# Issuing the loads of a cached attention kernel from GpSimd's DMA queue instead of SyncE's

## The chip, the core and the metric

The kernel runs on one core of one Trainium2 chip. The metric is the device time of one execution in microseconds, the median of several runs. A profile of one further execution says what each engine and each DMA queue did, and when. The engines are TensorE (PE; its weight loads are PEld), VectorE (DVE), ScalarE (ACT), GpSimd (POOL) and SyncE (SP), which here only issues DMAs.

## What is computed

One token attends over a cache of 65,536 keys and values for each of 8 key-value heads, with 2 query heads to each, and the result is mixed with a small MLP by a gate.

```python
q = (x @ wq).reshape(B, Sq, 16, 256)          # x is 1 x 448
scores = einsum(q, k_cache) * (256 ** -0.5)   # k_cache: 8 heads x 65536 x 256, bf16
a = (softmax(scores) @ v_cache).reshape(B, Sq, 4096) @ wo
h = layernorm(x)
b = gelu(h * w1 + b1) @ w2 + b2               # per channel, F = 1792
g = sigmoid((x * gate_w).sum(-1))
return g * a + (1 - g) * b
```

The two caches are 268 MB each and are read once; everything else is small.

## The kernel before

The 65,536 positions of each head are cut into 4 passes, so there are 32 passes (`NP`), four to a head (`PPH`). A pass takes 16,384 keys and the same number of values: 8 MB each, with 128 partitions and 64 KB of contiguous memory for each partition. A pass of keys is worked on in 8 steps (`BODY`) of 2,048 keys; the first four steps (`DC`) use the upper half of the keys' tile (`HV` to `NV`), the last four the lower half.

**The passes on TensorE.** In each step of `keys`, TensorE transposes 16 tiles of keys (line 359, `kst<-ident,kring`, as 32-bit pairs), VectorE (line 675) and ScalarE (line 820) copy them to `ktT`, and TensorE multiplies them with the query (line 380, `sps<-qcur,ktT`). The transposes count up `sem_tr`; `sem_tr[NB - 1]` is what the loads of keys wait for. After a pass's scores come the maximum (`maxima`, lines 397 and 399 on TensorE), the exponentials on ScalarE, and then `values` (line 411, `acc<-vbuf,pT`), 128 matmuls of weights with values, the last of which counts up `sem_pv`. In passes 0 and 1 the values of a pass are used right behind its keys; from pass 2 (`LEAD`) on, keys run one pass ahead of values. After four passes a head is finished: its output is multiplied with its part of wo (line 472, `project`, counting up `s_proj`).

**Buffers.** `kring` holds one pass of keys and a half, `vbuf` holds one pass of values. Before the first values arrive, `vbuf` holds wq and other early data, so that the first value load waits until the query is made (`s_q`, `s_hb`). Each later value load waits for the value matmuls before it (`sem_pv`), each key load for the transposes of the buffer half that it overwrites.

**Queues.** SyncE issues, in an order written out by hand in `block.sync`: the first wo, two pieces of wq, and both 4 MB halves of the first keys (`sem_k` for the upper half, `sem_kb` for the lower); then a loop over the passes with one load of keys and one of values in turn, a wo load after each finished head (`load_wo`, line 261), and at the end the last values in five pieces, the last wo in two and the store of the output. All cache loads go through one helper, `load`, whose DMA is line 269. Around `LEAD` the keys are loaded in halves and quarters, some with semaphores of their own (`sem_kc`, `sem_kq`). ScalarE issues six small loads at the start (lines 780 to 785). GpSimd makes the identity and the ones, then waits for the two quarter loads (`sem_kq`) and adds 16 to `sem_k` on their behalf.

**Waits on TensorE.** At the first step of a pass (`transposes`, `k == 0`, line 346) it waits for `sem_k` at 16 times the number of the pass; at the fifth step for `sem_kb` and, in three passes, for one of `sem_kc`. Before a projection it waits for `sem_wo`.

Of the kernel before, what the change touches and what calls it, by code (L numbers as in the profile page):

```python
# [7 lines left out]
AF = mybir.ActivationFunctionType  # L8
ALU = mybir.AluOpType
AX = mybir.AxisListType  # L10


def bass_gated_mix__gqa_block_cached__mixer_token_mlp__decode_kernel(
# [17 lines left out]
    H = A_k_cache.shape[1]  # L31
    T = A_k_cache.shape[2]
    DH = A_k_cache.shape[3]
    DM = A_x.shape[-1]
    HQ = A_wq.shape[1] // DH
    REP = HQ // H
# [9 lines left out]
    DC = 4  # L46
    NB = NT // 4
    NCPH = T // CH
    NC = H * NCPH
    BODY = 2 * DC  # L50
    NV = BODY * NT
    NP = NC // BODY
    PPH = NCPH // BODY
# [10 lines left out]
    LEAD = 2  # L64
    assert LEAD % 2 == 0 and 1 < LEAD < PPH
    NLATE = 112
    NRING = 72
    pieces = [(0, NRING), (NRING, 96), (96, NLATE), (NLATE, 124), (124, NV)]
# [16 lines left out]
    HV = NV // 2  # L85
# [11 lines left out]
    with ctx:  # L97
# [6 lines left out]
        def new_sem(name):  # L104
            return ctx.enter_context(nc.semaphore(name))

        kring = sb([P, NV + HV, DH], bf16, "kring")
        kring_f = kring.bitcast(f32)
        vbuf = sb([P, NV, DH], bf16, "vbuf")
# [10 lines left out]
        wo_sb = sb([P, REP, 2 * DM], bf16, "wo_sb")  # L120


        wo_rows = wo_sb[:, :, :].rearrange("p h n -> p (h n)")
# [73 lines left out]

        sem_k = new_sem("sem_k")
        sem_kb = new_sem("sem_kb")
        sem_kc = [new_sem("sem_kc%d" % i) for i in range(3)]  # L200
        sem_kq = [new_sem("sem_kq%d" % i) for i in range(2)]
        sem_v = new_sem("sem_v")
        sem_vp = [new_sem("semvp%d" % i) for i in range(len(pieces))]
# [3 lines left out]
        sem_wo = new_sem("sem_wo")  # L207
# [6 lines left out]
        sem_pv = new_sem("sem_pv")  # L214
# [37 lines left out]
        def src(cache, j, n0=0, n1=NV):  # L252
            g, m = divmod(j, PPH)
            s = cache[0, g, m * BODY * CH:(m + 1) * BODY * CH, :].rearrange("(p n) d -> p n d", p=P)
            return s[:, n0:n1, :].rearrange("p n d -> p (n d)")

        @block.sync
        def _(eng):
            def load_wo(g):
                w = A_wo[g * REP * DH:(g + 1) * REP * DH, :]  # L260
                eng.dma_start(wo_rows, w.rearrange("(p i) n -> p (i n)", i=2 * REP)).then_inc(sem_wo, 16)

            load_wo(0)
            eng.dma_start(wq_a.rearrange("p j n -> p (j n)"),
                          A_wq[0:WF * P, :].rearrange("(p j) n -> p (j n)", p=P)).then_inc(sem_wq, 16)
            eng.dma_start(wq_b, A_wq[WF * P:DM, :].rearrange("r (a n) -> (r a) n", a=2)
                          ).then_inc(sem_wq, 16)
            def load(dst, cache, j, n0, n1, at, sem):
                eng.dma_start(dst[:, at + n0:at + n1, :].rearrange("p n d -> p (n d)"), src(cache, j, n0, n1)
                              ).then_inc(sem, 16)  # L270

            load(kring, A_k_cache, 0, HV, NV, 0, sem_k)
            load(kring, A_k_cache, 0, 0, HV, 0, sem_kb)

            def load_v(j):
                if j == 0:
                    eng.wait_ge(s_q, 1)
                    eng.wait_ge(s_hb, 1)
                else:
                    eng.wait_ge(sem_pv, j)  # L280
                load(vbuf, A_v_cache, j, 0, NV, 0, sem_v)
                g, m = divmod(j, PPH)
                if m == 0 and 1 <= g < H - 1:
                    eng.wait_ge(s_proj, g)
                    load_wo(g)

            for j in range(NP):
                if j == LEAD + 1:
                    eng.wait_ge(sem_tr[NB - 1], BODY * LEAD)
                    load(kring, A_k_cache, j, HV, NV, HV, sem_kc[1])  # L290
                    eng.wait_ge(sem_tr[NB - 1], BODY * LEAD + DC // 2)
                    load(kring, A_k_cache, j, 0, HV // 2, HV, sem_kq[0])
                if j >= 1:
                    eng.wait_ge(sem_tr[NB - 1], BODY * (j - 1) + DC)
                if j == LEAD:
                    load(kring, A_k_cache, j, HV, NV, 0, sem_k)
                    load(kring, A_k_cache, j, 0, HV, 0, sem_kc[0])
                elif j == LEAD + 1:
                    load(kring, A_k_cache, j, HV // 2, HV, HV, sem_kq[1])
                elif j == NP - 1:  # L300
                    load(kring, A_k_cache, j, 0, HV, HV, sem_k)
                    load(kring, A_k_cache, j, HV, NV, HV, sem_kc[2])
                elif j >= 1:
                    load(kring, A_k_cache, j, 0, NV, HV * (j % 2), sem_k)
                if j < LEAD:
                    load_v(j)
                elif j > LEAD:
                    load_v(j - 1)


            for (n0, n1), sem in zip(pieces, sem_vp):
                if n0 == 0:
                    eng.wait_ge(sem_tr[NB - 1], BODY * (NP - 1) + DC)
                elif n0 == NRING:
                    eng.wait_ge(sem_pv, NP - 1)
                load(kring if n1 <= NRING else vbuf, A_v_cache, NP - 1, n0, n1, 0, sem)
            eng.wait_ge(s_proj, H - 1)
            for h in range(REP):
                w = A_wo[(HQ - REP + h) * DH:(HQ - REP + h + 1) * DH, :]
                eng.dma_start(wo_sb[:, h, :], w.rearrange("(p j) n -> p (j n)", j=2)).then_inc(sem_wl[h], 16)  # L320
            eng.wait_ge(s_fin, NCG)
            eng.dma_start(out_ap, out_row[:, :]).then_inc(sem_out, 16)
            eng.wait_ge(sem_out, 16)

        @block.gpsimd
        def _(eng):
            eng.memset(ident[:, :], 0.0)
            eng.drain()
            eng.affine_select(
                out=ident[:, :], in_=ident[:, :], compare_op=ALU.not_equal, fill=1.0,  # L330
                base=0, pattern=[[-1, P]], channel_multiplier=1,
            )
            eng.drain()
            eng.memset(ones_sq[:, :], 1.0).then_inc(sem_ident, 1)
            for sem in sem_kq:
                eng.wait_ge(sem, 16)
            eng.sem_inc(sem_k, 16)

        @block.tensor
        def _(pe):  # L340
# [2 lines left out]

            def transposes(k, c, j, u16, x2):
                if k == 0:
                    pe.wait_ge(sem_k, u16)
                if k == DC:
                    pe.wait_ge(sem_kb, 16)
                    for p, sem in zip((LEAD, LEAD + 1, NP - 1), sem_kc):
                        with pe.If(j == p):  # L350
                            pe.wait_ge(sem, 16)

                done = pe.snap(c + 1, min_val=1, max_val=NC)

                def tiles(at):
                    for b in range(NB):
                        pe.wait_ge(sem_ev[b], done)
                        for i in range(4):
                            ins = pe.transpose(kst[:, b, i * P:(i + 1) * P],  # L359
                                               kring_f[:, at + NT * (k % DC) + 4 * b + i, :], ident[:, :])  # L360
                        ins.then_inc(sem_tr[b], 1)

                if k < DC:
                    tiles(HV)
                else:
                    with pe.If(x2 == 0):
                        tiles(0)
                    with pe.Else():
                        tiles(NV)
# [165 lines left out]
            pe.reg_mov(m_reg, 0)  # L535
            g_reg = pe.alloc_register("g_reg")
            pe.reg_mov(g_reg, 1)
            with nc.Fori(0, NP + 1, 1, engines=on, head_slot={pe.engine: 0}) as jj:
                j = pe.snap(jj, min_val=0, max_val=NP)
                m = pe.snap(m_reg, min_val=0, max_val=PPH)  # L540
# [4 lines left out]
                    maxima(pe.snap(j, min_val=1, max_val=NP))  # L545
                with pe.If(j < NP):
                    c0 = pe.snap(j * BODY, min_val=0, max_val=NC)
                    u16 = pe.snap(j * 16 + 16, min_val=16, max_val=16 * NP)
                    keys(c0, j, u16, pe.snap(x2_reg, min_val=0, max_val=NV))
                with pe.Else():  # L550
                    pe.wait_ge(s_mix, 1)
# [16 lines left out]
                with pe.If(m >= PPH):  # L568
                    with pe.If(j < NP):
                        g1 = pe.snap(g - 1, min_val=1, max_val=H)  # L570
                        pe.wait_ge(s_cp, g1)
                        clear(acc[:, 0:NACC])
                        by_row(acc[:, SELC:NACC]).then_inc(s_sel, 1)
                        pe.wait_ge(sem_wo, pe.snap(g * 16 - 16, min_val=16, max_val=16 * H))
                        pe.wait_ge(s_oTn, g1)
                        project(range(2 * REP)).then_inc(s_proj, 1)
                        pe.reg_mov(m_reg, 0)
# [281 lines left out]
```

## Time and profile before

| | |
|---|---|
| runs | 1263.95, 1264.36, 1264.56 us; median 1264.36 us |
| span of the profiled execution (first to last instruction) | 1262.8 us |
| time of the profiled execution beside its span | not given on the page; its span stands 1.6 us below the median of the runs |
| mean granted TensorE clock | 0.842 |
| HBM read | 544.22 MB |
| DMA packets | 12,197, of which 1,433 are under 512 B |

The span is the profile's; the runs are timed as a whole. Rows of groups give the line, the engine, the operation, output and inputs, how often, the busy time with the mean duration, and the idle time before it with what ended it. Rows of waits give the total, the number and the longest. Rows of DMA issues give the transfer, the issuing queue, how often, the size where the page has it, and the median time from issue to landing. "x1" and the like is a count.

### The profile page before, as it was taken

To read this page: it belongs to the slowest core of one execution; us is meant where nothing else is said; L and a number is where in the kernel's file an instruction comes from. 1 tells how busy PE (TensorE), PEld (TensorE's weight loads), DVE (VectorE), ACT (ScalarE), POOL (GpSimd) and SP (SyncE) were. 2 spreads that over 40 slices of the span, in tenths; PEclk is the share of its full clock that TensorE was granted. 3 is DMA by queue.
4 is the path that set the end of the run, shared out by engine and by line. 5 is a ranking of instruction groups with operands and counts; after the bars stand their busy time and mean duration, and the time that the engine had idled before them with its cause. 6 is when DMAs were issued, how large, how long until landed. Compare 5 with 4: busy or idle time off the path is not lost.

```text
span 1262.8 us, 39606 instructions
## 1 busy us (share of the span) xinstructions
PE 974.4 (77%) x17019; PEld 891.1 (71%) x17019; DVE 498.3 (39%) x1126; ACT 545.7 (43%) x692; POOL 0.9 (0%) x7
## 2 busy tenths in 40 slices
PE   4768887678777797776977678886778866798787
PEld 3667876678667687666877667876668766687685
DVE  3234434344444435444354433342333432334342
ACT  2344643345433455343454334443344433445352
POOL 0000000000000000000000000000000000000000
PEclk8878888898877888788888889887798877888787
DMA  9999999999999999999999999999999999999998
GB/s 415 433 421 426 439 436 436 432 432 432 432 434 440 436 432 432 432 430 438 434 434 429 437 434 432 432 432 436 436 436 432 432 432 432 432 434 438 428 438 370
DMA packets 12197, 544.35 MB, mean 431 GB/s; under 512 B 1433, under 2 KB 1692, under 8 KB 2972
## 3 DMA queue, kind: packets, MB, share of 16 engines
q1 hardware_dynamic: 12098, 544.22, 99.8%
q8 instruction: 6, 0.10, 0.0%
q10 hardware_dynamic: 90, 0.01, 0.0%
q14 instruction: 3, 0.02, 0.0%
HBM read 544.22 MB, written 0.00 MB: 431 GB/s over the span
## 4 chain that ended last, share of the span: by engine, by line
DMA 58%; PE 37%; DVE 2%; issue 2%; DVEq 0%; SPq 0%; ACT 0%
DMA kring<-in_A_k_cache_dram 55%; PE kst L359 26%; PE sps L380 6%; PE acc L411 3%; DMA vbuf<-in_A_v_cache_dram 2%; DMA wo_sb<-in_A_wo_dram 1%; PE acc L461 0%; PE sps L399 0%; PE prj L472 0%; DVE ktT L675 0%; ACT z_b L825 0%; PE acc L404 0%; DVE accs L709 0%; PE sps L397 0%; DVE mrow L686 0%
## 5 line engine op out<-in xcount | busy, mean ns | idle before, releaser
L359 PE MATMUL kst<-ident,kring 128*128 128x128 f32 x4096 | 565.0, 299 | 181.4 <-DMA kring<-in_A_k_cache_dram 158.2
L359 PEld LDWEIGHTS kst<-ident,kring 128*128 128x128 f32 x4096 | 513.1, 156 | 190.7 <-issue 184.6
L820 ACT ACTIVATE ktT<-kst 128x1024 bf16<-128x1024 bf16 x512 | 499.9, 1021 | 337.2 <-PE kst L359 336.8
L675 DVE COPY ktT<-kst 128x1024 bf16<-128x1024 bf16 x512 | 353.9, 692 | 435.5 <-PE kst L359 409.4
L380 PEld LDWEIGHTS sps<-qcur,ktT 128*128 128x128 bf16 x8192 | 238.0, 97 | 2.6
L380 PE MATMUL sps<-qcur,ktT 128*128 128x2 bf16 x8192 | 236.6, 163 | 0.0
L411 PE MATMUL acc<-vbuf,pT 128*2 128x256 bf16 x4008 | 164.1, 341 | 4.6 <-issue 3.3
L411 PEld LDWEIGHTS acc<-vbuf,pT 128*2 128x2 bf16 x4008 | 113.5, 103 | 47.0 <-issue 4.5
L803 ACT ACTIVATE fade<-mdif 128x2 f32<-128x2 f32 x32 | 6.5, 203 | 305.1 <-DVE mdif L692 305.1
L686 DVE TENSOR_REDUCE mrow<-sps 2x1 f32<-2x128 f32 x32 | 8.9, 279 | 162.6 <-PE sps L397 162.6
L399 PEld LDWEIGHTS sps<-mdiag,mones 2*128 2x128 f32 x64 | 11.1, 216 | 27.9 <-DVE mdiag L688 27.9
L397 PE MATMUL sps<-ident,mcol 128*2 128x128 f32 x32 | 8.9, 279 | 27.9 <-issue 26.4
L399 PE MATMUL sps<-mdiag,mones 2*128 2x2 f32 x64 | 13.9, 284 | 21.3 <-DVE mdiag L688 21.3
L807 ACT ACTIVATE pT<-sps,mneg 128x64 f32 x128 | 30.3, 334 | 0.0
L825 ACT ACTIVATE z_b<-z_b 128x448 bf16<-128x448 bf16 x14 | 8.1, 576 | 48.2 <-DVE z_b L662 48.2
L404 PE MATMUL acc<-pT,ones_sq 128*128 128x32 bf16 x256 | 12.0, 182 | 21.9 <-issue 18.4
L397 PEld LDWEIGHTS sps<-ident,mcol 128*2 128x2 f32 x32 | 2.6, 80 | 36.6 <-issue 28.3
L709 DVE COPY accs<-acc 128x288 f32<-128x288 f32 x8 | 3.7, 458 | 61.7 <-PE acc L411 61.7
L681 DVE TENSOR_REDUCE mcol<-sps 128x2 f32<-128x256 f32 x32 | 13.5, 423 | 34.6 <-PE sps L380 34.6
L404 PEld LDWEIGHTS acc<-pT,ones_sq 128*128 128x128 bf16 x256 | 8.8, 99 | 26.0 <-issue 22.4
L704 DVE TENSOR_SCALAR acc<-acc,fader 128x256 f32<-128x256 f32 x32 | 15.8, 493 | 2.5
L691 DVE TENSOR_SCALAR mneg<-sps 128x2 f32<-128x2 f32 x32 | 5.1, 160 | 16.8 <-PE sps L399 16.8
(113 smaller groups left out, 168.8 us busy)
## 6 DMA issues: line engine op xcount, KB each, us to landing
kring<-in_A_k_cache_dram SPq DMA_DIRECT2D x7, 4096.0 KB, 25.2
kring<-in_A_v_cache_dram SPq DMA_DIRECT2D x1, 4608.0 KB, 25.4
kring<-in_A_k_cache_dram SPq DMA_DIRECT2D x2, 2048.0 KB, 13.1
wo_sb<-in_A_wo_dram SPq DMA_DIRECT2D x7, 448.0 KB, 25.3
vbuf<-in_A_wq_dram SPq DMA_DIRECT2D x1, 3072.0 KB, 10.8
vbuf<-in_A_v_cache_dram SPq DMA_DIRECT2D x1, 1536.0 KB, 8.1
vbuf<-in_A_v_cache_dram SPq DMA_DIRECT2D x1, 1024.0 KB, 10.2
vbuf<-in_A_v_cache_dram SPq DMA_DIRECT2D x1, 768.0 KB, 11.6
```

The source lines that it names most:

```text
L359: ins = pe.transpose(kst[:, b, i * P:(i + 1) * P], kring_f[:, at + NT * (k % DC) + 4 * b + i, :], ident[:, :])
L380: ins = pe.matmul(sps[:, 0, 2 * (NT * k + nt):2 * (NT * k + nt) + 2], ktT[:, par, b, ntl * DH + dj:(ntl + 1) * DH:2], qcur[:, dj, :], star ...
L397: pe.transpose(mxT, mcol[:, :], ident[:, :]).then_inc(s_mT, 1)
L399: pe.matmul(mxB, mones[:, :], mdiag[:, :], start=True, stop=True).then_inc(s_mB, 1)
L404: pe.matmul(acc[:, DENC:SELC], ones_sq[:, :], pT[:, r, :], start=False, stop=(r == BODY - 1), skip_group_check=True)
L411: ins = pe.matmul(acc[o:o + REP, 0:DH], pT[:, r, 2 * nt:2 * nt + 2], buf[:, n, :], start=False, stop=False, skip_group_check=True)
L675: vec.tensor_copy(ktT[:, k % KTB, b, :], kst_b[:, b, :]).then_inc(sem_ev[b], 1)
L681: vec.tensor_reduce(out=mcol[:, :], in_=scores_all.rearrange("p (n hh) -> p hh n", hh=REP), axis=AX.X, op=ALU.max)
L686: vec.tensor_reduce(out=mrow[:, :], in_=mxT, axis=AX.X, op=ALU.max)
L704: vec.tensor_scalar(acc[:, 0:DENC], acc[:, 0:DENC], fader[:, :], None, op0=ALU.mult).then_inc(s_acc, 1)
L807: ins = act.activation(pT[:, bass.ds(p0, DC), hh:2 * NT:REP], scores_all.rearrange("p (a r n hh) -> p a hh r n", a=2, r=DC, hh=REP)[:, hal ...
L820: act.activation(ktT[:, k % KTB, b, :], kst_b[:, b, :], AF.Copy).then_inc(sem_ev[b], 1)
```

## The change

SyncE keeps the first wo, wq, the two halves of the first keys and the final store. Every other load is issued by GpSimd, in the same order, behind the same waits, with the same shapes. GpSimd issues them behind its making of the identity.

Because a semaphore is now counted up by loads of one queue only, the first keys' upper half gets `sem_k0` and the first wo `sem_wo0`. TensorE's wait at the first step of a pass becomes three cases: pass 0 waits for `sem_k0`, pass 3 (`LEAD + 1`) for both `sem_kq`, all others for `sem_k` at a value held in a register, which they raise by 16. The wait for wo becomes two cases in the same manner. GpSimd no longer forwards `sem_kq` to `sem_k`. `HOW` is empty, so `**how` adds nothing.

```diff
+        def load(eng, dst, cache, j, n0, n1, at, sem, **how):
+            eng.dma_start(dst[:, at + n0:at + n1, :].rearrange("p n d -> p (n d)"), src(cache, j, n0, n1), **how
+                          ).then_inc(sem, 16)
...
         @block.sync
         def _(eng):
-            load_wo(0)
+            eng.dma_start(wo_rows, A_wo[0:REP * DH, :].rearrange("(p i) n -> p (i n)", i=2 * REP)
+                          ).then_inc(sem_wo0, 16)
...
-            load(kring, A_k_cache, 0, HV, NV, 0, sem_k)
-            load(kring, A_k_cache, 0, 0, HV, 0, sem_kb)
-
-            def load_v(j):
-                if j == 0:
-                    eng.wait_ge(s_q, 1)
-                    eng.wait_ge(s_hb, 1)
-                else:
-                    eng.wait_ge(sem_pv, j)
-                load(vbuf, A_v_cache, j, 0, NV, 0, sem_v)
...
-            for j in range(NP):
...
+            load(eng, kring, A_k_cache, 0, HV, NV, 0, sem_k0)
+            load(eng, kring, A_k_cache, 0, 0, HV, 0, sem_kb)
             eng.wait_ge(s_fin, NCG)
             eng.dma_start(out_ap, out_row[:, :]).then_inc(sem_out, 16)
             eng.wait_ge(sem_out, 16)
...
             eng.memset(ones_sq[:, :], 1.0).then_inc(sem_ident, 1)
-            for sem in sem_kq:
-                eng.wait_ge(sem, 16)
-            eng.sem_inc(sem_k, 16)
+            how = dict(HOW)
+
+            def load_v(j):
...
+                load(eng, vbuf, A_v_cache, j, 0, NV, 0, sem_v, **how)
...
+            for j in range(NP):
...
         @block.tensor
...
                 if k == 0:
-                    pe.wait_ge(sem_k, u16)
+                    with pe.If(j == LEAD + 1):
+                        for sem in sem_kq:
+                            pe.wait_ge(sem, 16)
+                    with pe.Else():
+                        with pe.If(j > 0):
+                            pe.wait_ge(sem_k, u16)
+                            pe.reg_add(u_reg, u_reg, 16)
+                        with pe.Else():
+                            pe.wait_ge(sem_k0, 16)
...
-                        pe.wait_ge(sem_wo, pe.snap(g * 16 - 16, min_val=16, max_val=16 * H))
+                        with pe.If(g > 2):
+                            pe.wait_ge(sem_wo, pe.snap(w_reg, min_val=16, max_val=16 * H))
+                            pe.reg_add(w_reg, w_reg, 16)
+                        with pe.Else():
+                            pe.wait_ge(sem_wo0, 16)
```

More of the change, by code (lines that the diff above doesn't have):

```diff
@@ L10 @@
 AX = mybir.AxisListType
+HOW = {}
 def bass_gated_mix__gqa_block_cached__mixer_token_mlp__decode_kernel(
@@ L199, in bass_gated_mix__gqa_block_cached__mixer_token_mlp__decode_kernel @@
         sem_kb = new_sem("sem_kb")
+        sem_k0 = new_sem("sem_k0")
+        sem_wo0 = new_sem("sem_wo0")
         sem_kc = [new_sem("sem_kc%d" % i) for i in range(3)]
@@ L255, in src, with load_wo @@
             return s[:, n0:n1, :].rearrange("p n d -> p (n d)")
+        def load(eng, dst, cache, j, n0, n1, at, sem, **how):
+            eng.dma_start(dst[:, at + n0:at + n1, :].rearrange("p n d -> p (n d)"), src(cache, j, n0, n1), **how
+                          ).then_inc(sem, 16)
+        def load_wo(eng, g, **how):
+            w = A_wo[g * REP * DH:(g + 1) * REP * DH, :]
+            eng.dma_start(wo_rows, w.rearrange("(p i) n -> p (i n)", i=2 * REP), **how).then_inc(sem_wo, 16)
         @block.sync
         def _(eng):
-            def load_wo(g):
-                w = A_wo[g * REP * DH:(g + 1) * REP * DH, :]
-                eng.dma_start(wo_rows, w.rearrange("(p i) n -> p (i n)", i=2 * REP)).then_inc(sem_wo, 16)
-            load_wo(0)
+            eng.dma_start(wo_rows, A_wo[0:REP * DH, :].rearrange("(p i) n -> p (i n)", i=2 * REP)
+                          ).then_inc(sem_wo0, 16)
             eng.dma_start(wq_a.rearrange("p j n -> p (j n)"),
@@ L267, in _ @@
                           ).then_inc(sem_wq, 16)
-            def load(dst, cache, j, n0, n1, at, sem):
-                eng.dma_start(dst[:, at + n0:at + n1, :].rearrange("p n d -> p (n d)"), src(cache, j, n0, n1)
-                              ).then_inc(sem, 16)
-            load(kring, A_k_cache, 0, HV, NV, 0, sem_k)
-            load(kring, A_k_cache, 0, 0, HV, 0, sem_kb)
-            def load_v(j):
-                if j == 0:
-                    eng.wait_ge(s_q, 1)
-                    eng.wait_ge(s_hb, 1)
-                else:
-                    eng.wait_ge(sem_pv, j)
-                load(vbuf, A_v_cache, j, 0, NV, 0, sem_v)
[L282 to L285, printed above, removed]
@@ L287, in _ @@
-            for j in range(NP):
[L288 to L308, printed above, removed]
@@ L311, in _ @@
[L311 to L320, printed above, removed]
+            load(eng, kring, A_k_cache, 0, HV, NV, 0, sem_k0)
@@ L334, in _ @@
             eng.memset(ones_sq[:, :], 1.0).then_inc(sem_ident, 1)
-            for sem in sem_kq:
-                eng.wait_ge(sem, 16)
-            eng.sem_inc(sem_k, 16)
+            how = dict(HOW)
+            def load_v(j):
+                if j == 0:
+                    eng.wait_ge(s_q, 1)
+                    eng.wait_ge(s_hb, 1)
+                else:
+                    eng.wait_ge(sem_pv, j)
+                load(eng, vbuf, A_v_cache, j, 0, NV, 0, sem_v, **how)
+                g, m = divmod(j, PPH)
+                if m == 0 and 1 <= g < H - 1:
+                    eng.wait_ge(s_proj, g)
+                    load_wo(eng, g, **how)
@@ new lines, in _ @@
+            for j in range(NP):
+                if j == LEAD + 1:
+                    eng.wait_ge(sem_tr[NB - 1], BODY * LEAD)
+                    load(eng, kring, A_k_cache, j, HV, NV, HV, sem_kc[1], **how)
+                    eng.wait_ge(sem_tr[NB - 1], BODY * LEAD + DC // 2)
+                    load(eng, kring, A_k_cache, j, 0, HV // 2, HV, sem_kq[0], **how)
+                if j >= 1:
+                    eng.wait_ge(sem_tr[NB - 1], BODY * (j - 1) + DC)
+                if j == LEAD:
+                    load(eng, kring, A_k_cache, j, HV, NV, 0, sem_k, **how)
+                    load(eng, kring, A_k_cache, j, 0, HV, 0, sem_kc[0], **how)
+                elif j == LEAD + 1:
+                    load(eng, kring, A_k_cache, j, HV // 2, HV, HV, sem_kq[1], **how)
+                elif j == NP - 1:
+                    load(eng, kring, A_k_cache, j, 0, HV, HV, sem_k, **how)
+                    load(eng, kring, A_k_cache, j, HV, NV, HV, sem_kc[2], **how)
+                elif j >= 1:
+                    load(eng, kring, A_k_cache, j, 0, NV, HV * (j % 2), sem_k, **how)
+                if j < LEAD:
+                    load_v(j)
+                elif j > LEAD:
+                    load_v(j - 1)
@@ new lines, in _ @@
+            for (n0, n1), sem in zip(pieces, sem_vp):
+                if n0 == 0:
+                    eng.wait_ge(sem_tr[NB - 1], BODY * (NP - 1) + DC)
+                elif n0 == NRING:
+                    eng.wait_ge(sem_pv, NP - 1)
+                load(eng, kring if n1 <= NRING else vbuf, A_v_cache, NP - 1, n0, n1, 0, sem, **how)
+            eng.wait_ge(s_proj, H - 1)
+            for h in range(REP):
+                w = A_wo[(HQ - REP + h) * DH:(HQ - REP + h + 1) * DH, :]
+                eng.dma_start(wo_sb[:, h, :], w.rearrange("(p j) n -> p (j n)", j=2), **how
+                              ).then_inc(sem_wl[h], 16)
@@ L537, in _ @@
             pe.reg_mov(g_reg, 1)
+            u_reg = pe.alloc_register("u_reg")
+            pe.reg_mov(u_reg, 16)
+            w_reg = pe.alloc_register("w_reg")
+            pe.reg_mov(w_reg, 16)
             with nc.Fori(0, NP + 1, 1, engines=on, head_slot={pe.engine: 0}) as jj:
@@ L547, in _ @@
                     c0 = pe.snap(j * BODY, min_val=0, max_val=NC)
-                    u16 = pe.snap(j * 16 + 16, min_val=16, max_val=16 * NP)
+                    u16 = pe.snap(u_reg, min_val=16, max_val=16 * NP)
                     keys(c0, j, u16, pe.snap(x2_reg, min_val=0, max_val=NV))
```

## The prediction

> **What bounds the kernel now.** I read the page first: its busy table, then the transfer rates over the 40 slices, then the queues.
>
> ```profile
> span 1262.8 us, 39606 instructions
> PE 974.4 (77%) x17019; PEld 891.1 (71%) x17019; DVE 498.3 (39%) x1126; ACT 545.7 (43%) x692; POOL 0.9 (0%) x7
> DMA  9999999999999999999999999999999999999998
> GB/s 415 433 421 426 439 436 436 432 432 432 432 434 440 436 432 432 432 430 438 434 434 429 437 434 432 432 432 436 436 436 432 432 432 432 432 434 438 428 438 370
> q1 hardware_dynamic: 12098, 544.22, 99.8%
> ```
>
> No compute engine is over 77%, but SyncE's queue (q1) keeps the 16 DMA engines busy for 99.8% of the span, at some 433 GB/s. The bound is bytes over DMA rate, so 1% of rate is worth 12.6 us. Anything else counts only where it leaves the DMA engines without a packet. Next come the waits of SyncE's queue, and TensorE's wait for keys.
>
> ```profile
> SPq L269 <- PE kst L359: 610.0, 34, 27.2
> SPq L269 <- PE acc L411: 572.7, 30, 28.7
> PE kst L359 <- DMA kring<-in_A_k_cache_dram: 158.2, 29, 9.5
> ```
>
> SyncE waits for freed buffers (transposes for keys, L411 for values); TensorE waits 5.5 us a pass for the next keys. So I measure the **lead** of an issue: how long before the landing of the load ahead of it. Issue times stand in the timeline of SyncE, times to landing in the DMA view of each window (columns: transfer, count, us to landing).
>
> ```profile
> 118.07 0.43 SPq L269 DMA_DIRECT2D vbuf<-in_A_v_cache_dram  x1
> 145.76 0.33 SPq L269 DMA_DIRECT2D kring<-in_A_k_cache_dram  x1
> ...
> 842.81 0.33 SPq L269 DMA_DIRECT2D kring<-in_A_k_cache_dram  x1
> 862.17 0.33 SPq L269 DMA_DIRECT2D vbuf<-in_A_v_cache_dram  x1
> ```
> ```profile
> vbuf<-in_A_v_cache_dram SPq DMA_DIRECT2D x1, 31.9
> ```
> ```profile
> kring<-in_A_k_cache_dram SPq DMA_DIRECT2D x1, 28.5
> ```
>
> The values issued at 118.07 land at 149.97; the keys behind them were issued at 145.76, a lead of 4.2 us, the shortest that I found. In mid-run the keys of 842.81 land at 871.3 and the next values were issued at 862.17: 9.1 us.
>
> **The change part by part.** (a) 79 loads (L269: 35 of keys and 36 of values; six of L261; two of L320) go to GpSimd, whose queue keeps the old order and waits. GpSimd is otherwise idle (0.9 us busy). No row shows a load issued by GpSimd. Its extra delay per load lies above nothing, since SyncE's own issue takes 0.33 us; up to 4.2 us the shortest lead hides it. I take 1 to 2 us, near SyncE's rows, hidden everywhere in steady state: zero. Without cover, each microsecond beyond the lead would cost some 60 us, one for each long load.
>
> The Trainium skill ("DMA: Bandwidth & Descriptors", latency and other measured facts) gives about 1 us to the first byte from GpSimd against 0.6 from SyncE. By that the term stays zero too.
>
> (b) **The hand-over.** wo, wq and both halves of the first keys (K0) stay on SyncE; the first values (V0) are the first load on the other queue. In one queue V0 began when K0 was done. Now both queues hold work at once.
>
> ```profile
> 2.13 1.00 SPq L269 DMA_DIRECT2D kring<-in_A_k_cache_dram  x2
> 19.55 0.33 SPq L269 DMA_DIRECT2D vbuf<-in_A_v_cache_dram  x1
> 33.93 0.33 SPq L269 DMA_DIRECT2D kring<-in_A_k_cache_dram  x1
> 63.02 0.33 SPq L269 DMA_DIRECT2D vbuf<-in_A_v_cache_dram  x1
> ```
> ```profile
> kring<-in_A_k_cache_dram SPq DMA_DIRECT2D x1, 4096.0 KB, 20.6
> ```
> ```profile
> kring<-in_A_k_cache_dram SPq DMA_DIRECT2D x2, 4096.0 KB, 25.7
> ```
> ```profile
> kring<-in_A_k_cache_dram SPq DMA_DIRECT2D x1, 38.5
> ```
>
> The first half (K0a) lands at 22.7. The 25.7 is the middle of 20.6 and 30.8, so the second half (K0b) lands near 33.4. V0 was issued at 19.55, with 13.9 us of K0 ahead of it; the next keys (K1) land at 72.4. How two queues share the engines, ScalarE's small loads (q10) show at the start: a window from 5.0 to 10.8 us, and the timeline.
>
> ```profile
> q1 hardware_dynamic: 111, 2.39, 95.9%
> q10 hardware_dynamic: 83, 0.01, 1.2%
> ```
> ```profile
> 2.85 0.32 ACTq L785 DMA_DIRECT2D b_b<-in_B_b_dram  x1
> ...
> 11.81 0.38 DVE L616 TENSOR_TENSOR vbuf<-vbuf 1x448 bf16<-1x448 bf16 x1 [5.80 <-DMA b_b<-in_B_b_dram]
> ```
>
> K0 was all queued by 3.13, ahead of the end of ScalarE's work, yet ScalarE's last load is in by 11.81, long before K0: not first come, first served. Nor do small loads pass first: 83 packets that need 1.2% of the time are spread among 111 large ones. That is packet about packet. The Trainium skill says so of a DMA engine with work from several queues ("DMA: Bandwidth & Descriptors", queues, rings and completion order); this row agrees.
>
> So packet sizes decide. Windows from 14 to 20 us (K0a) and from 650 to 690 us (full loads):
>
> ```profile
> q1 hardware_dynamic: 80, 2.62, 101.1%
> ```
> ```profile
> DMA packets 297, 17.37 MB, mean 434 GB/s; under 512 B 32, under 2 KB 32, under 8 KB 32
> ```
>
> K0: 2.62 MB / 80 = 32 KB a packet, 16 x 6 us / 80 = 1.2 us. Full loads: 17.37 MB / (297 - 32) = 64 KB, 2.4 us. These are the rows of a partition, and I take V0's and K1's packets from GpSimd to be the same 64 KB. With V0's first packet at about 21.5 (19.55 and the 1 to 2 us of (a), the upper end), K0 has 9 packets left on each engine: (22.7 - 21.5) / 1.2 = one of K0a, and 8 of K0b. Each waits for one of 2.4 us: 9 x (1.2 + 2.4) = 32.4, so **K0b lands near 54, not 33**. V0's eight are through at 21.5 + 8 x 2.4 + 7 x 1.2 = 49.1; K1, issued near 36, fills the turns behind. The sum of bytes is as before, so K1 still lands near 72.4.
>
> What is late next: TensorE cannot begin pass 0's second half before 54, and the second values (V1), until now issued at 63.02, 9.4 us ahead of K1's landing, wait for that pass's value matmuls. Pass 1 has the same steps:
>
> ```profile
> 72.51 6.62 PE L359 MATMUL kst<-ident,kring 128*128 128x128 f32 x32 [9.53 <-DMA kring<-in_A_k_cache_dram]
> 85.71 1.96 PE L359 MATMUL kst<-ident,kring 128*128 128x128 f32 x16 [0.64 <-issue]
> 101.52 5.74 PE L411 MATMUL acc<-vbuf,pT 128*2 128x256 bf16 x128
> 108.66 3.84 PE L359 MATMUL kst<-ident,kring 128*128 128x128 f32 x32 [1.40 <-issue]
> ```
> ```profile
> wo_sb<-in_A_wo_dram SPq DMA_DIRECT2D x1, 448.0 KB, 3.2
> ```
>
> From the second half's first transpose (85.71) to the last value matmul (101.52 + 5.74) are 21.6 us. After an idle stretch 32 transposes took 6.62 us, against 3.84: up to 2.8 more. V1 is thus issued between 75.6 and 78.4, with K1's data over at 72.4. An empty queue has its own delay: the first load (448 KB, 1.1 us of data) lands 3.2 us after its issue, so 2.1. V1's landing slips by (75.6 to 78.4) + 2.1 - 72.4 = 5.3 to 8.1 us; GpSimd's extra microsecond makes the upper end 9. I take 6.6, nearer the lower end, since the 21.6 is a row of the same steps. The DMA engines stand idle that long, and bytes are the bound, so the end moves as much. The stage behind has cover: TensorE starts pass 1 warm, in place of 6.62, and the next keys wait only for it.
>
> (c) TensorE's wait for keys gets two branches and a register add, its wait for wo one of each in seven projections. The ladder of four branches at the second half shows as 0.64 us of issue (row of 85.71). At most that per pass, beside a 5.5 us wait: zero; uncovered, 32 x 0.64 = 20 us.
>
> (d) GpSimd's forwarding of two semaphores goes, TensorE waits for both; a fraction of a microsecond off the path: zero. SyncE's final store waits as before.
>
> (e) The end.
>
> ```profile
> 1225.62 0.33 SPq L269 DMA_DIRECT2D kring<-in_A_v_cache_dram  x1
> 1246.66 1.75 SPq L269 DMA_DIRECT2D vbuf<-in_A_v_cache_dram  x4
> 1248.45 0.90 SPq L320 DMA_DIRECT2D wo_sb<-in_A_wo_dram  x2
> ```
> ```profile
> kring<-in_A_v_cache_dram SPq DMA_DIRECT2D x1, 4608.0 KB, 25.4
> ```
> ```profile
> wo_sb<-in_A_wo_dram SPq DMA_DIRECT2D x2, 224.0 KB, 11.9
> ```
>
> Six short loads are issued from 1246.66 with 4.4 us of lead (1225.62 + 25.4), and the last must be in the queue some 2 us before its landing near 1260.8: (1258.7 - 1246.7) / 6 = 2 us an issue are free. At 1 to 2 us: zero; at 3, 6 us.
>
> Sum: 6.6 us, all from (b). The span would be 1269.4. The page gives the profiled execution no time beside its span; the median of the runs, 1264.36, is 1.6 above it, and to that I add: **1271.0**.
>
> **The rivals.** *The hand-over is harmless* (not slower): V1 must be issued by 72.4 - 2.1 = 70.3, so K0b must land by 46 to 48.7. That holds if GpSimd's packets take at most (48.7 - 21.5)/9 - 1.2 = 1.8 us (49 KB), or if V0's first packet comes after about 25, for then 6 packets are left and 25.2 + 6 x 3.6 = 46.8. For: nothing shows a GpSimd load, and its first might start 5 us late. Against: SyncE's packets are one row each, and its delays are near 2 us. Time 1264 to 1266.
>
> *The rate falls* with the other queue. 0.5% costs 6.3 us, 1% 12.6, on top of the hand-over: 1277 to 1284 or more. Against: the same rows and the same engines. The Trainium skill calls two of the 16 engines usually slower and guesses at GpSimd's descriptor rings (same page, latency and other measured facts); no run here shows it.
>
> *GpSimd is too slow or blocked*: issues cost over 4.2 us, first felt at 145.76, then in mid-run beyond 7 to 9 us: from 1275 to far more. The Trainium skill ("SBUF — State Buffer", who interferes with whom) says that some VectorE instructions lock GpSimd out of descriptor writing. The longest from SBUF to SBUF in the loop is this one, in 14 passes of 32:
>
> ```profile
> L652 DVE TENSOR_SCALAR u_b<-wtmp,params 128x448 bf16<-128x448 bf16 x14 | 4.7, 336 | 2.6 <-issue 2.6
> ```
>
> A third of a microsecond, inside any lead.
>
> *The rate rises*, if that queue spends less between packets: at the 436 GB/s of good slices, 544.22 MB take 1248.2 us, and with some 2 us at each end the span falls by 10. It decides from 6.6 us up, 0.5% of rate: 1254 to 1262. Against: 99.8% is busy already.
>
> **How the numbers follow.** Hand-over 0.47 (1268 to 1274); harmless 0.24; lower rate 0.11; GpSimd too slow 0.06; higher rate 0.12. A measurement tells about 0.2% (2.5 us) from no change: faster 0.12, same 0.24, slower 0.64. The range from 1262 to 1284 holds the first two, half of the lower rate and a part of the higher.
>
> **What would show it.** Right: transposes of pass 0's second half start near 54, V1 is issued at 75 to 79, a dip in GB/s between 70 and 80 us, and slices at 432 to 436 behind it. Harmless: K0b's transposes by 48. Lower rate: every slice lower. Too slow: TensorE's waits for keys grow in all passes, and the DMA row drops below 9. Wrong altogether: V0's packets not alternating with K0's.

## The result, and the profile after

The changed kernel takes 1273.29 us (median of 4 runs, 1271.89 to 1274.93) against 1264.46 before (4 runs, 1263.95 to 1266.18): a ratio of 1.007, with a 95% interval from 1.0055 to 1.0084. That is 8.8 us slower, 0.7%. The profiled execution took 1274.31 us with a span of 1273.0, 10.2 us longer than the span before. From the page of the changed kernel come the span, the 40 slices and the queues (q0 is GpSimd's):

```profile
span 1273.0 us, 39745 instructions
...
DMA  9979999999999999999999999999999999999998
GB/s 407 440 299 421 444 428 430 441 428 430 428 428 443 428 428 449 439 412 455 432 428 430 441 428 430 428 429 443 428 428 453 418 432 449 432 430 430 428 428 377
...
q0 software_dynamic: 10768, 531.70, 96.7%
q1 hardware_dynamic: 722, 12.52, 2.3%
```

One slice stands out, the third (64 to 95 us) at 299 GB/s. The rest is much as before. The windows of the changed kernel locate it; the share of the DMA engines' time is the number before the last.

```profile
70.00:75.00 5.00, 3.28 (x66) 2.19 (x69) 1.29 (x7) 1.06 (x5) 0.00 (x0) 0.57 0.05 18
75.00:80.00 5.00, 3.43 (x80) 2.13 (x72) 0.00 (x0) 0.00 (x0) 0.53 (x1) 0.75 0.15 46
80.00:85.00 5.00, 3.21 (x15) 3.22 (x16) 1.05 (x2) 1.02 (x1) 0.00 (x0) 0.59 0.98 380
```

The DMA engines lose 5 x 0.95 + 5 x 0.85 = 9.0 us here. Before, these ten microseconds ran at 446 and 459 GB/s. What came ahead of the gap is in the timelines of TensorE and GpSimd in the changed kernel:

```profile
51.56 3.67 PE L370 MATMUL kst<-ident,kring 128*128 128x128 f32 x16 [15.02 <-issue]
...
55.92 3.65 PE L370 MATMUL kst<-ident,kring 128*128 128x128 f32 x16
...
64.56 1.95 PE L370 MATMUL kst<-ident,kring 128*128 128x128 f32 x16
...
72.21 6.22 PE L422 MATMUL acc<-vbuf,pT 128*2 128x256 bf16 x128
```
```profile
20.96 0.67 POOL L262 DMA_DIRECT2D vbuf<-in_A_v_cache_dram  x1 [19.13 <-DVE hbT L763]
36.07 0.53 POOL L262 DMA_DIRECT2D kring<-in_A_k_cache_dram  x1 [14.44 <-PE kst L370]
78.75 0.53 POOL L262 DMA_DIRECT2D vbuf<-in_A_v_cache_dram  x1 [42.15 <-PE acc L422]
```

TensorE stands still for 15 us until 51.56, then does the second half of pass 0, and the value matmuls end at 78.43. V1 is issued at 78.75, where it was 63.02, and finds the queue empty. Who took the turns meanwhile is in the queues' packets of the changed kernel, in windows from 20 to 25 us and from 25.1 to 43 us:

```profile
q1 hardware_dynamic: 80, 2.10, 97.2%
```
```profile
q0 software_dynamic: 80, 5.24, 68.1%
q1 hardware_dynamic: 77, 2.52, 32.6%
```

Up to 25 us GpSimd's queue has moved nothing. From then on, as long as every DMA engine still has packets of K0b, 80 packets of one queue go with 77 of the other. In MB that is 5.24 to 2.52, because GpSimd's packets are 64 KB and SyncE's 32 KB. K0b gets a third of the rate.

After the gap nothing more is lost. The long stretch from 300 to 1200 us, first the kernel before and then the changed one, moves 433 and 434 GB/s:

```profile
300.00:1200.00 900.00, 701.48 (x12282) 645.25 (x12280) 357.40 (x800) 393.02 (x498) 0.00 (x0) 0.84 1.00 433
```
```profile
300.00:1200.00 900.00, 695.39 (x12264) 641.14 (x12263) 357.39 (x800) 392.73 (x498) 26.98 (x51) 0.85 1.00 434
```

### The profile page after: what moved, and what is told of

The parts are those of the page before. It is cut to its first block, busy times and chain, and to the rows that moved or that the text cites. A ratio compares the mean times of both kernels' runs of the same rounds, so it can differ in the third digit from the quotient of the medians.

```text
span 1273.0 us, 39745 instructions
## 1 busy us (share of the span) xinstructions
PE 971.9 (76%) x17019; PEld 890.1 (70%) x17019; DVE 498.4 (39%) x1126; ACT 545.3 (43%) x692; POOL 42.8 (3%) x86
## 4 chain that ended last, share of the span: by engine, by line
DMA 60%; PE 35%; issue 3%; DVE 1%; DVEq 0%; POOL 0%; SPq 0%; ACT 0%
DMA kring<-in_A_k_cache_dram 57%; PE kst L370 26%; PE sps L391 6%; PE acc L422 3%; DMA vbuf<-in_A_v_cache_dram 2%; DMA wo_sb<-in_A_wo_dram 1%; PE acc L472 0%; PE sps L410 0%; POOL vbuf L262 0%; PE acc L415 0%; PE prj L483 0%; PE sps L408 0%; DVE ktT L694 0%; DVE mrow L705 0%; DVE mcol L700 0%
## 5 line engine op out<-in xcount | busy, mean ns | idle before, releaser
L370 PE MATMUL kst<-ident,kring 128*128 128x128 f32 x4096 | 565.4, 300 | 196.6 <-DMA kring<-in_A_k_cache_dram 156.2
L262 POOL DMA_DIRECT2D vbuf<-in_A_v_cache_dram x35 | 18.6, 532 | 598.0 <-PE acc L422 578.9
L262 POOL DMA_DIRECT2D kring<-in_A_k_cache_dram x35 | 18.5, 528 | 589.3 <-PE kst L370 589.3
## 6 DMA issues: line engine op xcount, KB each, us to landing
kring<-in_A_k_cache_dram SPq DMA_DIRECT2D x2, 4096.0 KB, 34.8
```

Of the source, the lines that this page charges most:

```text
L370: ins = pe.transpose(kst[:, b, i * P:(i + 1) * P], kring_f[:, at + NT * (k % DC) + 4 * b + i, :], ident[:, :])
```

## The experiments

The theory is the hand-over: two queues take turns packet by packet, K0b falls behind V0, and V1 is issued late. The rivals are GpSimd's issue as such (each load starts later, or its queue runs slower), TensorE's new branches and waits, and a sharing by bytes. From the trace of the changed kernel, V0's first packet comes near 25.2 us, and the slowest DMA engine then has seven turns before it, six with data and one with the small packet that raises the semaphore. All runs are compared with the kernel before on the same chip.

**All loads back on SyncE.** The new semaphores and branches stay; only the issuing engine changes.

```diff
         @block.sync
...
+            for j in range(NP):
...
             eng.wait_ge(s_fin, NCG)
             eng.dma_start(out_ap, out_row[:, :]).then_inc(sem_out, 16)
...
         @block.gpsimd
...
-            for j in range(NP):
...
```

> The changed kernel with all its new semaphores and TensorE branches, but SyncE issues every load again. If the loss comes from the hand-over between two queues, or from GpSimd's issue, there is no second queue left and the time is that of before: 1263.5 to 1266 us, with the second half of pass 0's transposes starting near 35 us. If it comes from TensorE's new branches and waits, the time stays near 1273 us.

Measured: 1264.45 us, a ratio of 1.0001 (0.9991 to 1.0011). TensorE's second half starts as before:

```profile
34.60 1.96 PE L370 MATMUL kst<-ident,kring 128*128 128x128 f32 x16 [0.57 <-issue]
```

TensorE's branches and the split semaphores cost nothing. The loss comes with the second queue.

**V0's packets made smaller.** V0 stays one load of the same bytes from GpSimd. Only the length of its rows changes: 16 KB, 32 KB and 8 KB.

```diff
-                load(eng, vbuf, A_v_cache, j, 0, NV, 0, sem_v, **how)
+                load(eng, vbuf, A_v_cache, j, 0, NV, 0, sem_v, **(dict(max_dma_last_dim=16384) if j == 0 else how))
```

> The changed kernel, but the first value load (V0) is cut into rows of 16 KB in place of 64 KB, still one load of the same bytes from GpSimd. Hand-over by packets in turn: with V0's first packet near 25.2 us and seven turns left on the slowest DMA engine, each turn costs 1.2 + 0.6 us in place of 1.2 + 2.4, so K0b ends near 25.2 + 7 x 1.8 = 38 and TensorE's second half starts at 38 to 40 us (51.6 in the changed kernel). V0 still lands near 53, V1 is issued near 63 as in before, no gap at 70 to 80, and the time is 1263.5 to 1266. If GpSimd's slower issue as such is the cost, or if the queues share by bytes and not by packets, nothing moves: second half near 51, 1272 to 1275 us.

> The same with rows of 32 KB for V0. Hand-over by packets: 25.2 + 7 x (1.2 + 1.2) = 42 us, and one turn more for the semaphore packet: TensorE's second half starts at 42 to 45. From there to the last value matmul 21.6 us (warm) to 26.9 (as in the changed kernel, slow clock): V1 is issued at 64 to 72, K1 ends at 71.5, so the gap is 0 to 2 us and the time 1264 to 1267. Sharing by bytes, or GpSimd's issue as such: as the changed kernel, 1272 to 1275.

> As with V0 in rows of 16 KB, but 8 KB: seven turns of 1.2 + 0.3 us from 25.2 end near 36, TensorE's second half starts at 36 to 38 us. If the 0 to 3 us that the 16 KB kernel still loses in most runs come from V1's and the next loads' thin leads (V1 issued at 66.7 there, 63.0 in the kernel before), this gives them 2 us more lead: 1264 to 1266, with few runs over 1266. If they come from something that GpSimd's queue does later, at any lead, the same spread stays, 1264.2 to 1267.7.

The second half's first transposes on TensorE and V1's issue on GpSimd, with 32 KB, with 16 KB and with 8 KB:

```profile
43.41 3.67 PE L370 MATMUL kst<-ident,kring 128*128 128x128 f32 x16 [8.45 <-issue]
73.72 0.53 POOL L262 DMA_DIRECT2D vbuf<-in_A_v_cache_dram  x1 [38.67 <-PE acc L422]
```
```profile
38.90 3.31 PE L370 MATMUL kst<-ident,kring 128*128 128x128 f32 x16 [3.86 <-issue]
66.74 0.53 POOL L262 DMA_DIRECT2D vbuf<-in_A_v_cache_dram  x1 [31.62 <-PE acc L422]
```
```profile
36.66 1.96 PE L370 MATMUL kst<-ident,kring 128*128 128x128 f32 x16 [1.12 <-issue]
64.62 0.53 POOL L262 DMA_DIRECT2D vbuf<-in_A_v_cache_dram  x1 [29.00 <-PE acc L422]
```

| V0's rows | expected start of second half | measured | V1 issued | median us | ratio to before |
|---|---|---|---|---|---|
| 64 KB (changed kernel) | 54 (prediction) | 51.56 | 78.75 | 1273.29 | 1.007 (1.0055 to 1.0084) |
| 32 KB | 42 to 45 | 43.41 | 73.72 | 1269.10 | 1.0038 (1.0025 to 1.005) |
| 16 KB | 38 to 40 | 38.90 | 66.74 | 1267.36 | 1.0017 (1.0006 to 1.0027) |
| 8 KB | 36 to 38 | 36.66 | 64.62 | 1265.38 | 1.001 (1.0001 to 1.0019) |

The three starts with shorter rows lie in the ranges given for turns by packet (with 64 KB, seven turns of 3.6 us from 25.2 end at 50.4). Sharing by bytes is out, and so is GpSimd's issue as such, under which nothing would have moved. With 32 and 16 KB, V1 came later than expected (64 to 72, and near 63), and the medians lie 2.1 and 1.4 us above the upper ends of their ranges. From the start of the second half to V1 TensorE took 30 and 28 us, not the 22 to 27 assumed. In both, it stands still amid the value matmuls, for 4.20 and 3.57 us, and the trace shows no releaser:

```profile
70.26 3.15 PE L422 MATMUL acc<-vbuf,pT 128*2 128x256 bf16 x55 [4.20 <-issue]
```
```profile
63.28 3.15 PE L422 MATMUL acc<-vbuf,pT 128*2 128x256 bf16 x55 [3.57 <-issue]
```

**K0b's packets made smaller.** The opposite dose: twice as many packets on SyncE's side, each of which waits its turn.

```diff
-            load(eng, kring, A_k_cache, 0, 0, HV, 0, sem_kb)
+            load(eng, kring, A_k_cache, 0, 0, HV, 0, sem_kb, max_dma_last_dim=16384)
```

> The changed kernel, but the second half of the first keys (K0b), on SyncE's queue, is cut into rows of 16 KB in place of 32 KB: twice as many packets, each of which waits for one 64 KB packet of GpSimd's queue. Hand-over by packets: 14 turns of 0.6 + 2.4 us from 25.2 us end near 68 us, TensorE's second half starts at 66 to 71, V1 is issued some 27 us later, near 93 to 98, and the DMA engines, done with V0 and K1 near 71.5, stand idle for 22 to 27 us: 1286 to 1291 us. GpSimd's issue as such, or sharing by bytes: the 9 us of the changed kernel stay, 1272 to 1275.

Measured: 1285.57 us (1284.01 to 1292.04), a ratio of 1.0186 (1.0159 to 1.0213). The timeline has the second half at 66.20 after 31 us of standing still, and V1 at 88.49; the window from 75 to 80 us is empty:

```profile
66.20 3.30 PE L370 MATMUL kst<-ident,kring 128*128 128x128 f32 x16 [31.25 <-issue]
...
70.14 1.95 PE L370 MATMUL kst<-ident,kring 128*128 128x128 f32 x16
...
88.49 0.53 POOL L262 DMA_DIRECT2D vbuf<-in_A_v_cache_dram  x1 [53.47 <-PE acc L422]
```
```profile
75.00:80.00 5.00, 4.10 (x99) 3.81 (x96) 2.07 (x5) 2.77 (x3) 0.00 (x0) 1.00 0.02 3
```

The start lies in the range (66 to 71). V1 followed after 22 us and not 27, so that the time is a little under the 1286 expected. Nothing was changed but the length of the rows of a load that GpSimd does not issue, and 12 us more were lost: GpSimd's issue as such can't explain that.

**No overlap at all.** GpSimd issues V0 only when K0b has landed; in a second kernel when three steps of pass 0 are transposed.

```diff
                     eng.wait_ge(s_hb, 1)
+                    eng.wait_ge(sem_kb, 16)
```
```diff
                     eng.wait_ge(s_hb, 1)
+                    eng.wait_ge(sem_tr[NB - 1], 3)
```

> The changed kernel, but GpSimd waits for K0b's semaphore before it issues V0, so that the two queues never hold work at once. Hand-over by packets: K0b is back at 33.4 us, TensorE's second half starts at 34 to 36, V1 is issued with a lead, and the gap at 70 to 80 us is gone. In its place the DMA engines run dry between K0b's last packets (about 31.5 to 33) and V0's first one, which comes 1.2 to 4.2 us after an issue near 34 (V1's and V0's first packets in the changed kernel): 3.5 to 6.5 us lost, 1268 to 1271 us. If the loss were GpSimd's issue at V1 as such, the gap at 70 to 80 would stay and the two would add up: 1276 us or more.

> The changed kernel with V0 in full 64 KB rows, but GpSimd issues it only when three steps of pass 0 are transposed (near 30.7 us, before K0b's last packets at 31.5 to 33), so that V0's first packet comes at 32 to 35. Hand-over by packets: at most one turn of K0b is disturbed, TensorE's second half starts at 34 to 37, and the DMA engines run dry for 0 to 3 us instead of the 4 us of waiting for K0b's semaphore: 1264.5 to 1267.5. A cost of GpSimd's queue that does not depend on the overlap would leave 1270 or more.

Measured: 1269.73 us (ratio 1.0044, 1.0029 to 1.0058) and 1267.70 us (1.0025, 1.0016 to 1.0034). In the first, TensorE's second half is back at 34.47; the window from 32 to 34 us is dry and the one from 70 to 75 is full:

```profile
34.47 1.97 PE L371 MATMUL kst<-ident,kring 128*128 128x128 f32 x16 [0.50 <-issue]
```
```profile
32.00:34.00 2.00, 1.96 (x43) 1.86 (x41) 1.37 (x2) 1.59 (x2) 0.00 (x0) 1.00 0.00 0
70.00:75.00 5.00, 0.00 (x0) 0.00 (x0) 0.00 (x0) 0.00 (x0) 0.00 (x0) 0.50 1.17 501
```

So the gap at 70 to 80 us is the overlap's. What is left, 5.4 and 3.3 us, fits DMA engines that run dry before V0's first packet. In the second kernel the second half starts at 36.05, as expected (34 to 37), but V0 was issued at 32.88, later than the 30.7 assumed; its time lies just above the range's end, 2 us less than the first, of which 1.2 are the earlier issue (34.05 there).

**TensorE kept busy while it waits for K0b.** 96 transposes of the identity, which nothing reads, are added.

```diff
                 if k == DC:
+                    with pe.If(j == 0):
+                        for _ in range(96):
+                            pe.transpose(sps[:, 1, 3 * P:4 * P], ident[:, :], ident[:, :])
                     pe.wait_ge(sem_kb, 16)
```

> The changed kernel, but while TensorE waits for K0b in pass 0 it makes 96 transposes of the identity into a free part of a PSUM bank, which nothing reads. K0b still comes at 51 us. If the 26.9 us from the second half's first transpose to V1's issue are 5 us longer than pass 1's because TensorE's clock had dropped in its idle stretch, they come back to 21.6 to 23, V1 is issued at 73 to 75, and the gap shrinks from 9 us to 3 to 5: 1267 to 1270 us. If the slow start has nothing to do with idleness, the time stays at 1272 to 1275.

Measured: 1273.51 us (1270.33 to 1275.37), ratio 1.0071 (1.0052 to 1.009). That is no change, the time expected if idleness plays no part. The timeline of TensorE shows more:

```profile
34.96 10.68 PE L361 MATMUL sps<-ident 128*128 128x128 f32 x96
51.70 3.67 PE L373 MATMUL kst<-ident,kring 128*128 128x128 f32 x16 [6.06 <-issue]
...
56.03 1.95 PE L373 MATMUL kst<-ident,kring 128*128 128x128 f32 x16
...
65.25 1.61 PE L394 MATMUL sps<-qcur,ktT 128*128 128x2 bf16 x56 [1.92 <-issue]
```

The clock is part of it: with 6 us of idleness in place of 15, only the first 16 transposes are slow (3.67 us), where three groups were; the granted clock is back at 1.00 from 56 us, where the changed kernel has 0.50 up to 60. But the length of the idleness does not set this: with K0b's rows of 16 KB, TensorE stood still for 31 us, and there too only the first 16 were slow (3.30 us). Here TensorE also stood still for 1.92 us until 65.25, for which the trace shows no releaser. V1 came at 77.59, 1.2 us earlier than in the changed kernel, not the 4 to 6 expected. The clock alone does not explain the long way from K0b to V1.

**V0 too on SyncE.** The hand-over is then between V0 and K1, with 64 KB on both sides.

```diff
+            eng.wait_ge(s_q, 1)
+            eng.wait_ge(s_hb, 1)
+            load(eng, vbuf, A_v_cache, 0, 0, NV, 0, sem_v0)
             eng.wait_ge(s_fin, NCG)
...
                 if j == 0:
-                    eng.wait_ge(s_q, 1)
-                    eng.wait_ge(s_hb, 1)
-                else:
-                    eng.wait_ge(sem_pv, j)
+                    return
+                eng.wait_ge(sem_pv, j)
```

> The changed kernel, but V0 too stays on SyncE's queue (with a semaphore of its own), so that the first load on GpSimd is K1. Hand-over by packets: K0b is unharmed (second half at 34 to 36 us), but now V0 shares with K1, 64 KB against 64 KB: with K1's first packet at 36 to 39 and six or seven of V0's eight packets left, V0 ends 7 x 4.84 us later, near 70, its value matmuls near 77 to 82, and V1 finds the DMA engines idle since 71.5: a gap of 6 to 12 us, 1270 to 1277. If only K0b's delay, or something about V0, were at fault, this kernel would be at 1264 to 1266.

Measured: 1271.51 us, ratio 1.0059 (1.0043 to 1.0076). K0b is unharmed, the values now come late, and V1 with them (timelines of TensorE and GpSimd):

```profile
35.24 1.96 PE L372 MATMUL kst<-ident,kring 128*128 128x128 f32 x16 [0.52 <-issue]
...
68.00 3.67 PE L424 MATMUL acc<-vbuf,pT 128*2 128x256 bf16 x72 [14.47 <-DMA vbuf<-in_A_v_cache_dram]
```
```profile
75.00 0.54 POOL L263 DMA_DIRECT2D vbuf<-in_A_v_cache_dram  x1 [40.07 <-PE acc L424]
```

The loss is not tied to K0b. In both kernels the load that is half through on the old queue, and needed, is thinned out by the first load on the new one.

**The rest with 16 KB rows.** Runs of that kernel lie between 1264.24 and 1267.73 us. In its trace the DMA engines ran low only where pass 4's keys are issued; here their lower half goes out as soon as pass 2 is through.

```diff
+                if j == LEAD + 2:
+                    eng.wait_ge(sem_tr[NB - 1], BODY * (j - 1))
+                    load(eng, kring, A_k_cache, j, 0, HV, 0, sem_kc[3], **how)
...
+                elif j == LEAD + 2:
+                    load(eng, kring, A_k_cache, j, HV, NV, 0, sem_k, **how)
```

> V0 in rows of 16 KB as before, and the keys of pass 4 in two halves: the lower one is issued as soon as pass 2 is through, some 16 us earlier, the upper one where the whole was. In the profile of the kernel with 16 KB rows alone, the only stretch where the DMA engines ran dry after 3 us and before the end is 147.7 to 150 us (0.9 us lost), right where these keys are issued at 148.0. If that thin lead is what keeps its runs between 1264.2 and 1267.7, all runs are now at 1264 to 1265. If it is something else, the spread up to 1267.7 stays.

Measured: 1266.08 us (1264.46 to 1267.40 in 10 runs), ratio 1.0013 (1.0003 to 1.0023). The spread stays, so that this one thin lead is not its cause. With 8 KB rows the median falls to 1265.38, but four of 11 runs are still above 1266. Where these last 0 to 3 us go is open.

No version beats the kernel before, and there is little room for one: its DMA engines are idle only at the two ends.

## Why the prediction was right

It said 1271.0 us for 1273.29, a loss of 6.6 for 8.8, and named the place: the DMA engines idle before V1.

*The hand-over (b)* holds: packet about packet (80 to 77), smaller and larger packets on either side, and the two kernels without overlap. K0b, issued near 2.6, landed at 50.5, where the prediction had 54 (in the DMA view the two halves have a median of 34.8 us, the first 21.7, hence 47.9 for the second):

```profile
kring<-in_A_k_cache_dram SPq DMA_DIRECT2D x1, 4096.0 KB, 21.7
```
```profile
kring<-in_A_k_cache_dram SPq DMA_DIRECT2D x2, 4096.0 KB, 34.8
```

Two errors nearly cancel in that number, and that is luck. V0's first packet came after 25 us, not at 21.5, so that about six packets were left to wait, not nine; by the prediction's own working K0b would then have landed at 46.8. But the packet that raises the semaphore takes a turn too. In the window from 43 to 47 us, 13 of these 16 small packets go out, and the last three only between 47 and 50.5. One more turn of 3.6 us makes 50.4. The rows of the two windows:

```profile
DMA packets 46, 2.03 MB, mean 508 GB/s; under 512 B 13, under 2 KB 13, under 8 KB 13
```
```profile
q1 hardware_dynamic: 3, 0.00, 0.0%
```

The harmless rival set its limit at a first packet after about 25 us, without this turn. The changed kernel was at that limit and paid in full.

*The size.* The prediction's 6.6 was V1's issue at 76.9, plus 2.1 for an empty queue, less 72.4. Measured: V1 was issued at 78.75 and landed 22.9 us later, of which 19.3 are data by the spacing of the landings before; so 3.6, not 2.1. That gives 78.75 + 3.6 - 72.4 = 9.95 us for the profiled execution, whose span is 10.2 us longer than before (the medians differ by 8.8).

```profile
vbuf<-in_A_v_cache_dram POOLq DMA_DIRECT2D x1, 22.9
```

Three terms were too small, and K0b's landing, 3.5 us earlier than predicted, hides half of that. TensorE's second half began 1.1 us behind that landing, where the prediction had no delay. The way from there to V1 took 27.2 us, where pass 1 had 21.6, the 76.9 stands for 22.9, and the prediction allowed at most 24.4: three groups of transposes took 3.65 us in place of 1.95, at a granted clock of 0.50 (50 to 60 us). And the GpSimd load into an empty queue took 1.5 us more beyond its data than the SyncE load that the 2.1 came from. Only 0.2 of that lies ahead of the first packet, which came 1.2 us behind the issue (78.75 to 79.97), with SyncE 1.0 (0.74 to 1.77); the rest was not taken apart. The four make -3.5 + 1.1 + 4.3 + 1.5 = 3.4, the step from 6.6 to 9.95.

*The zeros.* (a) The rate from 300 to 1200 us is the same, and the whole delay is there at V1's landing: 101.65 for 91.72, 9.9 us. The last pieces are issued 9.96 us later than before (1246.66), with GpSimd's six issues taking 3.2 us in all:

```profile
1256.62 2.10 POOL L262 DMA_DIRECT2D vbuf<-in_A_v_cache_dram  x4 [20.87 <-PE acc L422]
1258.71 1.07 POOL L339 DMA_DIRECT2D wo_sb<-in_A_wo_dram  x2
```

So the steady state and the end (e) cost nothing. (c) and (d) are shown to be free by the kernel with all loads on SyncE. Of the other rivals, neither a lower nor a higher rate appeared, and TensorE's wait for keys did not grow (156.2 us in all, 158.2 before). The cover behind the gap held: nothing more was lost, and nothing came back. It was thinner than the prediction had it, for TensorE did not start pass 1 warm: it stood still for 3.35 us without a releaser, and its first 32 transposes took 6.59 us.

```profile
81.79 6.59 PE L370 MATMUL kst<-ident,kring 128*128 128x128 f32 x32 [3.35 <-issue]
```

The next keys were issued at 93.85, still 7.8 us ahead of V1's landing.

Open is the spread of the changed kernel's own runs (3 us, where the kernel before has under 2.3).

## What to carry to other kernels

In these runs, moving part of a stream of loads to a second queue cost nothing in rate (433 and 434 GB/s), but it ended first come, first served: where both queues held work, each packet of one waited for a packet of the other (80 to 77), so that the share went by the sizes of the packets, and the load with the smaller ones starved. Before such a change, list what is still in flight on the old queue when the new one starts, who waits for it, and what that waiter must do before the next load can be issued. The hand-over was cheap where the first load on the new queue had short rows (8 KB: 1 us). Waiting until the old queue had sent what was needed still cost 3.3 to 5.4 us, for the DMA engines ran dry. A hand-over at a place where nothing on the old queue is needed soon was not run.

## What was not expected

GpSimd's first load needed over 4 us from its issue (20.96) to its first packet (near 25.2), though V1, issued into idle DMA engines, needed 1.2. That it is the first does not explain it: in the two kernels without overlap V0 is GpSimd's first load too, and its first packet came 1.4 us behind the issue (34.05 to 35.4, and 32.88 to 34.3), with the other queue through or nearly so. With V0 on SyncE, GpSimd's first load is K1, issued while SyncE's queue still held work, and it took 4.2 us again (34.26 to 38.5). The packets ahead were 64 KB there and 32 KB in the changed kernel, so the delay is not a fixed number of packets. It comes with work on the other queue; by what way is open.

TensorE has short idle stretches without a releaser in pass 0, where it goes through its loop for the first time, or right behind it (the 3.35 us above): before, 3.3 us in the middle of the value matmuls (waits of TensorE, 35 to 64 us). Beside them the trace has packets of a queue for instructions (q8): four of 16 KB between 36 and 60 us before, one in the changed kernel, in the same window.

```profile
PE acc L411 <- issue: 3.3, 1, 3.3
```
```profile
q8 instruction: 4, 0.07, 1.1%
```
```profile
q8 instruction: 1, 0.02, 0.3%
```

The view counts them among the packets of the same 16 engines as the data, so that they may have to wait their turn as well, and pass 0 would then be slower than the passes after it. That is not shown, and was not tried.
